# The first batch of an attention in chunks of 512, 288 and 288 tokens, and what of it stands ahead of the expert work

## The chip, the cores and the metric

The kernel runs on one core of a Trainium2 chip. The metric is the device time of one execution in microseconds (us). The parts of the core that matter here are TensorE (PE in the profile, with its weight loads as PEld), VectorE (DVE), ScalarE (ACT), GpSimd (POOL) and the queue of SyncE (SP), from which the transfers are issued. All data are float32.

## The reference

A polynomial-sketch attention feeds a mixture of eight experts whose weights come from eight rounds of Sinkhorn normalisation. Cut to what matters:

```python
def phi(x):                       # x: 4 batches, 4 heads, 1088 tokens, 32
    a = einsum('rd,bhsd->bhsr', S1, x)         # r = 8
    b = einsum('rd,bhsd->bhsr', S2, x)
    return einsum('bhsi,bhsj->bhsij', a, b)    # 64 features
q_p, k_p = phi(q), phi(k)
kv  = einsum('bhsf,bhsd->bhfd', k_p, v)        # over all keys of a batch
z   = sum(k_p, axis=2)
num = einsum('bhsf,bhfd->bhsd', q_p, kv)
den = einsum('bhsf,bhf->bhs', q_p, z)[..., None] + 1e-6
x   = num / den                                # 4352 tokens x 128
P   = exp(x @ w_gate - max), then 8 times: rows and columns normalised
out = sum over e of P[:, e] * (relu(x @ w1[e]) @ w2[e])   # 8 experts, 128 -> 1024 -> 128
```

The queries of a batch can be worked through in chunks of tokens, once the sums `kv` and `z` over all its keys are there. The experts' first products on a token need only that token's `x`; the router's weights `P` need all tokens.

## The kernel before

**The attention.** For each batch b, `transpose_k` and `transpose_q` (L276, L272) turn keys and queries with DVE transposes; `keys_ab` (L285), `keys_products` (three DVE products, L301) and `keys_sums` (72 small matmuls, L314) make the key sums, and `keys_kept` (L331) copies these from PSUM to the tile kvz in four small copies, by ACT and DVE in turn. The queries go in three chunks of 384, 352 and 352 tokens (`chunks`, L344). A chunk passes four functions: `query_products` (PE: eight matmuls on half the rows of the array each; ACT: two copies to qa), `multiply` (DVE: two products, L367), `fractions` (PE: eight matmuls into two banks, pd first and then pn, L377), and `divide` (DVE, in a row: a transpose of pd, an addition, a reciprocal, a transpose back, and the product with pn that writes the chunk's part of xT; L389 to L396).

**The expert work.** `steps()` (L979) is a generator. One of its steps is a first product (L800: four matmuls, of up to 480 tokens) with its relu on ACT (L804). Four steps are a block of two slices of the hidden layer by two tiles of tokens. Strassen's scheme with seven products replaces eight second products: in the first step of the next block DVE makes a double subtraction, in the step after that two single ones (`two`, L817), and from eight steps on (`LAG`, L767) the second products follow (L967: four matmuls a step). Steps 0 to 15 work on the first group of tokens, 0 to 511 of batch 0, in two tiles of 256 that take turns (`groups`, L531): even steps use tokens 0 to 255, odd ones 256 to 511. Step 16 starts the next group, of two tiles of 480 tokens: 512 to 991, and 992 to 1471, which reaches into batch 1.

**What sets the order.** The attention is written out by hand among the expert work. `fill(n)` (L1037) adds n to a debt and takes steps while it is over 0.25; a step of 256 tokens pays 256/480, one of 480 tokens pays 1:

```python
def fill(n):
    owed[0] += n
    while owed[0] > 0.25:
        owed[0] -= next(work)
```

In the first hand-written part (L1042 to L1061) DVE, PE and ACT take their work in the order of the code. From L1064 on this holds for DVE and PE alone; ACT, POOL and the queue of SP are put in order by the planner of the framework, as are the buffers. The four PSUM buffers of `bank()` (L94) serve the key sums, the fractions and the first products in turn; the query products of batch 0 use the four banks of the second products instead (L270). The weights of the first expert, w1 and w2, are loaded early (`first_w`, L262) on the queue of SP, behind keys, queries and values of batch 0 and the keys and queries of batch 1; the values of batch 1 come behind them.

Before the change, L1042 to L1091 take, per fill, these steps: 0 and 1; 2 and 3; 4 and 5; 6 and 7; 8; 9 and 10; 11 and 12; 13 and 14; then in `attention(1)` (L413) 15 and 16; and from 17 on one step per fill.

Of the kernel before, what the change touches and what calls it, by code (L numbers as in the profile page):

```python
# [10 lines left out]
F32 = mybir.dt.float32  # L11
# [39 lines left out]
def kernel(  # L51
# [13 lines left out]
    P = nc.NUM_PARTITIONS  # L65
    B, H, S, D = q.shape
# [25 lines left out]
    wk = early.enter_context(tc.tile_pool(name="wk", bufs=2))  # L92

    def bank():  # L94
        return aps.tile([P, 512], F32, tag="a", name="a")
# [141 lines left out]
    def projections():  # L237
        flat = raw.rearrange("p n d -> p (n d)")
        s12 = f64_to_f32(nc, consts, flat, (P, 2 * D)) if words == 2 else flat.bitcast(F32)
        st = consts.tile([P, 2, 32], F32, name="st")  # L240
        nc.vector.transpose(out=st.rearrange("p n r -> p (n r)"), in_=s12)
        nc.vector.tensor_tensor(wd, st[:, :, 0:R].unsqueeze(2).to_broadcast([P, 2, H, R]),
                                own.unsqueeze(1).unsqueeze(3).to_broadcast([P, 2, H, R]), op=Alu.mult)
        return st

    def repeated(st):
        for s in range(2):
            one = half[:, s:s + 1].unsqueeze(2).to_broadcast([P, R, R])
            nc.vector.tensor_tensor(wq[:, 0, s], st[:, 0, 0:R].unsqueeze(2).to_broadcast([P, R, R]), one, op=Alu.mult)
            nc.vector.tensor_tensor(wq[:, 1, s], st[:, 1, 0:R].unsqueeze(1).to_broadcast([P, R, R]), one,  # L250
                                    op=Alu.mult)
# [16 lines left out]
    def products_bank(b, i):  # L268

        return bank() if b else mps.tile([P, 512], F32, tag=f"s{i}", name="s")  # L270

    def transpose_q(b, lo=0, hi=S):  # L272
        if not lo:
            queries[b] = wk.tile([P, S], F32, tag="qT", name="qT")
        nc.vector.transpose(out=queries[b][:, lo:hi], in_=loaded[b][1].rearrange("p a d -> p (a d)")[:, lo:hi])  # L275

    def transpose_k(b):
        kx = loaded[b][0]
        kT = wk.tile([P, S], F32, tag="kT", name="kT")
        nc.vector.transpose(out=kT[:, 0:NT * P].rearrange("p (t c s) -> p c t s", c=4, s=32),  # L280
                            in_=kx[:, 0:4 * NT, :].rearrange("p (c t) d -> p c t d", c=4))
        nc.vector.transpose(out=kT[:, NT * P:S], in_=kx[:, 4 * NT:SA, :].rearrange("p a d -> p (a d)"))
        keys[b] = kT

    def keys_ab(b):  # L285

        kT = keys[b]
        ab = wk.tile([P, 2, NT + 1, H * R], F32, tag="ab", name="ab")
        pk = bank().rearrange("p (t n f) -> p t n f", t=NT, n=2)
        for t in range(NT):  # L290
            for s in range(2):
                sl = slice(64 * s, 64 * (s + 1))
                nc.tensor.matmul(pk[sl, t].rearrange("p n f -> p (n f)"), kT[:, P * t + 64 * s:P * t + 64 * (s + 1)],  # L293
                                 wdf, start=True, stop=True, tile_position=(0, 64 * s))
        nc.scalar.copy(ab[:, :, 0:NT, :], pk.rearrange("p t n f -> p n t f"))
        pr = bank()[0:64, 0:2 * H * R]
        nc.tensor.matmul(pr, kT[:, NT * P:S], wdf, start=True, stop=True, tile_position=(0, 0))
        nc.scalar.copy(ab[0:64, :, NT, :], pr.rearrange("p (n f) -> p n f", n=2))
        keys[b] = ab
# [31 lines left out]
    def keys_kept(b):  # L331
        pv = sums_of.pop(b)

        kvz = summed[b % 2]
        for i in range(2):
            for s in range(2):
                sl = slice(64 * s, 64 * (s + 1))
                if s:
                    nc.vector.tensor_copy(kvz[sl, :, i, s, :], pv[sl, i])
                else:  # L340
                    nc.scalar.copy(kvz[sl, :, i, s, :], pv[sl, i])
        keys[b] = kvz

    chunks = ((0, 384), (384, 736), (736, S))  # L344

    def query_products(b, c):

        lo, hi = chunks[c]
        n = hi - lo
        qT = queries[b]  # L350
        banks = [[products_bank(b, 2 * i + m) for m in range(2)] for i in range(2)]
        for m in range(2):
            for i in range(2):
                sl = slice(64 * i, 64 * (i + 1))
                nc.tensor.matmul(banks[i][m][:, 0:n], wqf[sl, m, :], qT[sl, lo:hi], start=True, stop=True,  # L355
                                 tile_position=(64 * i, 0))
        ph = []
        for i in range(2):
            qa = wk.tile([P, 384], F32, tag=f"qa{i}", name="qa")
            nc.scalar.copy(qa[:, 0:n], banks[i][0][:, 0:n])  # L360
            ph.append((qa, banks[i][1]))
        queries[b, c] = ph

    def multiply(b, c):
        n = chunks[c][1] - chunks[c][0]
        for qa, pb in queries[b, c]:
            nc.vector.tensor_tensor(qa[:, 0:n], qa[:, 0:n], pb[:, 0:n], op=Alu.mult)  # L367

    def fractions(b, c):

        n = chunks[c][1] - chunks[c][0]
        kvz = keys[b]
        ph = queries[b, c]
        pn, pd = bank(), bank()
        for t, m in ((pd, 1), (pn, 0)):
            for i in range(2):
                nc.tensor.matmul(t[64 * i:64 * (i + 1), 0:n], kvz[:, (i + m) % 2, i].rearrange("p h d -> p (h d)"),  # L377
                                 ph[i][0][:, 0:n], start=True, stop=True, tile_position=(0, 64 * i))
        queries[b, c] = pn, pd

    def divide(b, c):


        lo, hi = chunks[c]
        n = hi - lo
        nb = n // 32
        pn, pd = queries.pop((b, c))
        rd = wk.tile([P, 384], F32, tag="rd", name="rd")
        nc.vector.transpose(out=rd[:, 0:n], in_=pd[:, 0:n])  # L389
        rc = wk.tile([P, 12], F32, tag="rc", name="rc")[:, 0:nb]  # L390
        nc.vector.tensor_scalar_add(rc, rd[:, 0:n].rearrange("p (b r) -> p b r", r=32)[:, :, 0], 1e-6)
        nc.vector.reciprocal(rc, rc)
        rd = wk.tile([P, 384], F32, tag="rd", name="rd")
        nc.vector.transpose(out=rd[:, 0:n].rearrange("p (b r) -> p b r", r=32),
                            in_=rc.unsqueeze(2).to_broadcast([P, nb, 32]))
        nc.vector.tensor_tensor(xT[:, b * S + lo:b * S + hi], pn[:, 0:n], rd[:, 0:n], op=Alu.mult)  # L396
# [640 lines left out]
# [5 lines that stand above are left out]
    with tc.manual_schedule(engines={engines.DVE, engines.PE, engines.Activation}):  # L1042
        st = projections()
        transpose_k(0)
        keys_ab(0)
        repeated(st)
        transpose_q(0, 0, chunks[0][1])
        query_products(0, 0)
        for part_ in range(3):
            keys_products(0, part_)  # L1050
        keys_sums(0)
        multiply(0, 0)
        transpose_q(0, chunks[0][1])
        keys_kept(0)
        query_products(0, 1)
        fractions(0, 0)
        multiply(0, 1)
        divide(0, 0)
        fractions(0, 1)
        query_products(0, 2)  # L1060
        divide(0, 1)  # L1061
    counts = {1: (1, 1, 1, 1, 1, 1, 1, 1, 1), 2: (1, 1, 1, 1, 1, 1, 1, 1, 1, 1, 1, 2),
              3: (1, 1, 1, 1, 1, 1, 1, 1, 1, 1, 1, 1.25)}
    with tc.manual_schedule(engines={engines.DVE, engines.PE}):  # L1064
        fill(1)
        multiply(0, 2)
        fractions(0, 2)
        fill(1)
        transpose_k(1)
        divide(0, 2)  # L1070
        keys_ab(1)
        fill(1)
        transpose_q(1)
        load_kq(2)
        load_v(2)
        fill(1)
        keys_products(1, 0)
        query_products(1, 0)
        fill(1)
        keys_products(1, 1)  # L1080
        multiply(1, 0)
        fill(1)
        keys_products(1, 2)
        keys_sums(1)
        transpose_k(2)
        fill(1)
        keys_kept(1)
        fractions(1, 0)
        fill(1)
        for b in range(1, B):  # L1090
            for n, _ in zip(counts[b], attention(b), strict=True):  # L1091
                fill(n)
        for n in routing():
            fill(n)
        early.close()
        pools.append(ctx.enter_context(tc.tile_pool(name="late", bufs=2)))
        prepare_x(PLAIN)
        fill(8)
# [32 lines left out]
```

## Time and profile before

| | |
|---|---|
| median of four runs | 944.72 us (944.17 to 945.11) |
| the profiled execution | 944.47 us, of which the profile's span is 942.7 us |
| PE busy | 928.8 us (99%) |
| DVE busy | 702.8 us (75%) |
| ACT busy | 419.1 us (44%) |
| POOL busy | 192.5 us (20%) |
| TensorE clock granted, mean | 0.999 |

Times in the profile count from the span's start. In a line of the timeline the first number is the start, the second the duration (of a merged group, what it kept its engine busy), then engine, line, operation, tiles and shape; in brackets stands the engine's idle time before it and what ended that. A matmul's end is modelled and includes its way through the array, so two matmuls in a row overlap in the record, and the pace is read from starts. In a view by windows each entry is an engine's busy time in that stretch with its instructions in brackets, then the granted clock, the share of the DMA engines and their rate.

### The profile page before, as it was taken

What the parts mean: (1) busy time and instruction counts of PE and PEld (TensorE: products, weight loads), DVE (VectorE), ACT (ScalarE), POOL (GpSimd) and SP (SyncE); (2) the same over time, 40 slices, a digit from 0 to 9 for tenths busy, and PEclk for the clock granted to TensorE, in tenths of its full rate; (3) what the DMA queues carried; (4) which work ended last, traced back from release to release, by engine and by line L of the source; (5) the groups of instructions that cost most, each with busy time, mean ns of one, the idle gap of its engine ahead of it and who ended that gap; (6) DMA issues with size and microseconds to landing.
All of it is one profiled execution on the core that took longest, in us unless ns stands there. A gap on an engine that the chain in (4) does not pass through costs nothing.

```text
span 942.7 us, 18269 instructions
## 1 busy us (share of the span) xinstructions
PE 928.8 (99%) x7170; PEld 591.2 (63%) x7170; DVE 702.8 (75%) x1214; ACT 419.1 (44%) x894; POOL 192.5 (20%) x176
## 2 busy tenths in 40 slices
PE   8999999999999999999999999999999999999996
PEld 6553535566666666666666666666666666667864
DVE  7787579987778778676885756975767976668664
ACT  2444445555444454444544444544445444445443
POOL 2000000072456511040011100200110333311210
PEclk9999999999999999999999999999999999999999
DMA  6600000212434474444353434354344455443640
GB/s 191 188 1 1 2 1 1 68 62 85 129 107 124 121 237 130 144 142 159 122 154 116 169 128 130 124 164 149 120 132 139 155 175 185 155 168 92 188 131 12
DMA packets 86342, 113.07 MB, mean 120 GB/s; under 512 B 23888, under 2 KB 67920, under 8 KB 81904
## 3 DMA queue, kind: packets, MB, share of 16 engines
q1 hardware_dynamic: 85024, 111.74, 37.8%
q8 instruction: 56, 0.92, 0.4%
q10 hardware_dynamic: 1232, 0.16, 0.1%
q14 instruction: 30, 0.25, 0.1%
HBM read 99.03 MB, written 12.85 MB: 119 GB/s over the span
## 4 chain that ended last, share of the span: by engine, by line
PE 93%; DVE 5%; issue 1%; ACT 0%; DMA 0%; DVEq 0%; ACTq 0%
PE a L800 48%; PE s L967 41%; PE a L355 1%; PE a L377 1%; DVE hb L817 1%; PE a L324 1%; DVE hx L817 0%; DVE hx L862 0%; PE a L293 0%; DVE kp L309 0%; DMA raw<-in_S_dram 0%; DVE qa L367 0%; DVE kT L280 0%; DVE qT L275 0%; PE a L402 0%
## 5 line engine op out<-in xcount | busy, mean ns | idle before, releaser
L800 PE MATMUL a<-xe,w 128*64 128x256 f32 (+1 forms) x2560 | 525.6, 470 | 0.0
L804 ACT ACTIVATE hb<-a 128x256 f32<-128x256 f32 (+3 forms) x392 | 192.1, 492 | 257.6 <-PE a L800 232.6
L800 PEld LDWEIGHTS a<-xe,w 128*64 128x64 f32 x2560 | 227.6, 137 | 57.8
L804 ACT ACTIVATE hx<-a 128x256 f32<-128x256 f32 (+1 forms) x360 | 167.1, 464 | 213.0 <-PE a L800 192.6
L967 PE MATMUL s<-hb,ws 128*64 128x256 f32 (+2 forms) x1312 | 239.8, 400 | 0.0
L967 PE MATMUL s<-hx,ws 128*64 128x256 f32 x1280 | 209.3, 379 | 1.6 <-ACT f L679 1.1
L862 DVE TENSOR_TENSOR hb<-hb 128x512 f32<-128x512 f32 (+1 forms) x204 | 134.0, 666 | 101.1 <-ACT hb L804 96.7
L569 POOL TENSOR_TENSOR xe<-xT,xe 128x768 f32<-128x768 f32 (+2 forms) x41 | 84.2, 2054 | 567.5 <-DMA xe<-pT 387.3
L862 DVE TENSOR_TENSOR hx<-hx 128x512 f32<-128x512 f32 (+1 forms) x204 | 152.5, 756 | 62.0 <-ACT hx L804 56.8
L967 PEld LDWEIGHTS s<-hb,ws 128*64 128x64 f32 x1312 | 119.3, 137 | 101.7 <-issue 79.8
L967 PEld LDWEIGHTS s<-hx,ws 128*64 128x64 f32 x1280 | 116.1, 137 | 90.4 <-issue 67.4
L800 PE MATMUL a<-xT,w 128*64 128x480 f32 (+2 forms) x448 | 121.7, 506 | 1.1 <-DVE xT L396 0.9
L967 PE MATMUL s<-hb,w 128*64 128x256 f32 (+2 forms) x472 | 101.8, 423 | 1.0 <-DVE kept L627 1.0
L817 DVE TENSOR_TENSOR hb<-hb 128x480 f32<-128x480 f32 (+5 forms) x84 | 66.5, 795 | 13.8 <-PE s L967 7.2
L967 PE MATMUL s<-hx,w 128*64 128x256 f32 x384 | 69.6, 379 | 0.1
L800 PEld LDWEIGHTS a<-xT,w 128*64 128x64 f32 x448 | 44.2, 137 | 33.1 <-issue 18.1
L225 POOL TENSOR_TENSOR ws<-w 128x256 f32<-128x256 f32 (+1 forms) x70 | 60.4, 897 | 13.9 <-PE a L800 9.5
L967 PEld LDWEIGHTS s<-hb,w 128*64 128x64 f32 x472 | 44.9, 137 | 26.0 <-issue 11.6
L817 DVE TENSOR_TENSOR hx<-hx 128x256 f32<-128x256 f32 (+1 forms) x65 | 39.6, 614 | 24.3 <-ACT hx L804 17.9
L862 DVE TENSOR_TENSOR pqg<-hb 128x512 f32<-128x512 f32 x68 | 49.6, 770 | 0.0
L967 PEld LDWEIGHTS s<-hx,w 128*64 128x64 f32 x384 | 36.8, 137 | 8.0 <-DVE hx L817 0.5
L862 DVE TENSOR_TENSOR pqg<-hx 128x512 f32<-128x512 f32 x68 | 34.9, 553 | 0.0
(150 smaller groups left out, 484.4 us busy)
## 6 DMA issues: line engine op xcount, KB each, us to landing
w<-in_moe_w_dram SPq DMA_DIRECT2D x82, 512.0 KB, 5.4
ws<-ws SPq DMA_DIRECT2D x34, 1024.0 KB, 5.1
xe<-pT SPq DMA_DIRECT2D x34, 384.0 KB, 3.9
ws<-ws SPq DMA_DIRECT2D x12, 512.0 KB, 4.4
pb<-pT SPq DMA_DIRECT2D x6, 384.0 KB, 6.5
kx<-in_k_dram SPq DMA_DIRECT2D x4, 544.0 KB, 4.0
qx<-in_q_dram SPq DMA_DIRECT2D x4, 544.0 KB, 5.8
v<-in_v_dram SPq DMA_DIRECT2D x32, 64.0 KB, 4.5
```

The lines of the kernel that those rows point to most:

```text
L225: tc.keep_in_program_order(nc.gpsimd.tensor_tensor(ws[:, c:c + len(ns)], blocks(x), blocks(y), op=Alu.subtract if off else Alu.add))
L324: nc.tensor.matmul(pv[64 * s:64 * (s + 1), i], kp[0:n, H * t + h].rearrange("p i j -> p (i j)"), vx[0:n, slots[h], t, :], start=(t == 0 an ...
L355: nc.tensor.matmul(banks[i][m][:, 0:n], wqf[sl, m, :], qT[sl, lo:hi], start=True, stop=True, tile_position=(64 * i, 0))
L377: nc.tensor.matmul(t[64 * i:64 * (i + 1), 0:n], kvz[:, (i + m) % 2, i].rearrange("p h d -> p (h d)"), ph[i][0][:, 0:n], start=True, stop=T ...
L569: tc.keep_in_program_order(nc.gpsimd.tensor_tensor(out, x, pb, op=Alu.mult))
L800: nc.tensor.matmul(ph[sl], loaded_w[j][0][:, P * f + H2 * s:P * f + H2 * (s + 1)], sources[j][:, lo:hi], start=True, stop=True, tile_posit ...
L804: nc.scalar.activation(out=out, in_=ph, func=Act.Relu)
L817: nc.vector.tensor_tensor(out, a, b, op=Alu.subtract)
L862: nc.vector.tensor_tensor(out if not isinstance(out, tuple) else places(*out), places(*a), places(*b) if isinstance(b, tuple) else b, op=A ...
L967: nc.tensor.matmul(sums[g][i][H2 * s:H2 * (s + 1), n * place:n * (place + 1)], w, x, start=c == 1, stop=c == per, tile_position=(0, H2 * s))
```

## The change

Batch 0 gets chunks of its own: 512, 288 and 288 tokens instead of 384, 352 and 352. The other batches keep theirs. So `divide(0, 0)` now gives all of tokens 0 to 511, on which the first sixteen steps work.

In the first hand-written part, chunk 0 goes through to its `divide` with nothing of the other chunks between but the transpose of their queries and the query products of chunk 1; `fractions(0, 0)` now stands ahead of these query products on PE. The multiplication of chunk 1, its fractions and division, the query products of chunk 2 and the rest move into the second part, with fills between them. The fills ahead of `keys_ab(1)` are 0.5, 1, 0.5 and 0.5 instead of 1 and 1. Where the first query products and the division use tiles of 384 columns, these become 512 wide.

```diff
     chunks = ((0, 384), (384, 736), (736, S))
+    first_chunks = ((0, 512), (512, 800), (800, S))
+
+    def chunk(b, c):
+        lo, hi = (chunks if b else first_chunks)[c]
+        return lo, hi, hi - lo
...
-            qa = wk.tile([P, 384], F32, tag=f"qa{i}", name="qa")
+            qa = wk.tile([P, 512], F32, tag=f"qa{i}", name="qa")
...
-        rd = wk.tile([P, 384], F32, tag="rd", name="rd")
+        rd = wk.tile([P, 512], F32, tag="rd", name="rd")
...
-        transpose_q(0, 0, chunks[0][1])
+        transpose_q(0, 0, 512)
         query_products(0, 0)
         for part_ in range(3):
             keys_products(0, part_)
         keys_sums(0)
         multiply(0, 0)
-        transpose_q(0, chunks[0][1])
         keys_kept(0)
+        fractions(0, 0)
+        transpose_q(0, 512)
         query_products(0, 1)
-        fractions(0, 0)
-        multiply(0, 1)
         divide(0, 0)
-        fractions(0, 1)
-        query_products(0, 2)
-        divide(0, 1)
...
     with tc.manual_schedule(engines={engines.DVE, engines.PE}):
+        multiply(0, 1)
+        fill(0.5)
+        fractions(0, 1)
+        query_products(0, 2)
         fill(1)
+        divide(0, 1)
         multiply(0, 2)
+        fill(0.5)
         fractions(0, 2)
-        fill(1)
+        fill(0.5)
         transpose_k(1)
         divide(0, 2)
         keys_ab(1)
```

What follows `keys_ab(1)` is unchanged: six fills of 1 up to `attention(1)`.

More of the change, by code (lines that the diff above doesn't have):

```diff
@@ L344 @@
     chunks = ((0, 384), (384, 736), (736, S))
+    first_chunks = ((0, 512), (512, 800), (800, S))
+    def chunk(b, c):
+        lo, hi = (chunks if b else first_chunks)[c]
+        return lo, hi, hi - lo
     def query_products(b, c):
-        lo, hi = chunks[c]
-        n = hi - lo
+        lo, hi, n = chunk(b, c)
         qT = queries[b]
@@ L364, in multiply @@
     def multiply(b, c):
-        n = chunks[c][1] - chunks[c][0]
+        lo, hi, n = chunk(b, c)
         for qa, pb in queries[b, c]:
@@ L369, in fractions @@
     def fractions(b, c):
-        n = chunks[c][1] - chunks[c][0]
+        lo, hi, n = chunk(b, c)
         kvz = keys[b]
@@ L381, in divide @@
     def divide(b, c):
-        lo, hi = chunks[c]
-        n = hi - lo
+        lo, hi, n = chunk(b, c)
         nb = n // 32
         pn, pd = queries.pop((b, c))
-        rd = wk.tile([P, 384], F32, tag="rd", name="rd")
+        rd = wk.tile([P, 512], F32, tag="rd", name="rd")
         nc.vector.transpose(out=rd[:, 0:n], in_=pd[:, 0:n])
-        rc = wk.tile([P, 12], F32, tag="rc", name="rc")[:, 0:nb]
+        rc = wk.tile([P, 16], F32, tag="rc", name="rc")[:, 0:nb]
         nc.vector.tensor_scalar_add(rc, rd[:, 0:n].rearrange("p (b r) -> p b r", r=32)[:, :, 0], 1e-6)
         nc.vector.reciprocal(rc, rc)
-        rd = wk.tile([P, 384], F32, tag="rd", name="rd")
+        rd = wk.tile([P, 512], F32, tag="rd", name="rd")
         nc.vector.transpose(out=rd[:, 0:n].rearrange("p (b r) -> p b r", r=32),
```

## The prediction

> **What bounds the kernel now.** I read the page first, by slices and by the chain that ended last.
>
> ```profile
> PE   8999999999999999999999999999999999999996
> ...
> PEclk9999999999999999999999999999999999999999
> ...
> PE 93%; DVE 5%; issue 1%; ACT 0%; DMA 0%; DVEq 0%; ACTq 0%
> ```
>
> PE sets the time, at a full clock; its work is the same after the change (the same matmuls over the same columns). So the change can move the time only by PE's breaks, and nearly all breaks but the tail's are in the first slices. There I took the windows and PE's waits from 6 to 45 us:
>
> ```profile
> 18.00:20.00 2.00, 1.32 (x10) 0.38 (x6) 1.79 (x5) 1.19 (x3) 0.00 (x0) 1.00 0.54 119
> 26.00:28.00 2.00, 0.68 (x8) 0.38 (x6) 2.00 (x3) 0.62 (x2) 0.00 (x0) 1.00 0.86 268
> 36.00:38.00 2.00, 1.69 (x10) 1.02 (x11) 1.62 (x5) 0.20 (x1) 0.00 (x0) 1.00 0.92 275
> 80.00:100.00 20.00, 20.00 (x162) 9.54 (x161) 13.32 (x23) 10.41 (x21) 0.00 (x0) 1.00 0.01 1
> ...
> PE a L355 <- DVE qT L275: 1.3, 1, 1.3
> PE a L800 <- DVE xT L396: 0.9, 1, 0.9
> PE s L355 <- DVE qT L275: 0.5, 1, 0.5
> ```
>
> PE idles in the first three windows, while DVE is full (2.00 of 2.00 at 26 to 28); from 40 us on PE is full. So up to about 28 us DVE carries the chain, and PE waits for it. The timeline of DVE:
>
> ```profile
> 11.31 1.00 DVE L367 TENSOR_TENSOR qa<-qa,s 128x384 f32<-128x384 f32 x2
> 12.24 0.90 DVE L275 STREAM_TRANSPOSE qT<-qx 128x704 f32<-128x704 f32 x1
> 14.80 0.95 DVE L367 TENSOR_TENSOR qa<-qa,s 128x352 f32<-128x352 f32 x2 [0.92 <-PE s L355]
> 15.67 0.58 DVE L389 STREAM_TRANSPOSE rd<-a 128x384 f32<-128x384 f32 x1
> 17.91 0.54 DVE L389 STREAM_TRANSPOSE rd<-a 128x352 f32<-128x352 f32 x1
> 20.04 0.94 DVE L367 TENSOR_TENSOR qa<-qa,s 128x352 f32<-128x352 f32 x2
> 20.90 1.24 DVE L280 STREAM_TRANSPOSE kT<-kx 128x1024 f32<-128x1024 f32 x1
> 26.10 1.30 DVE L275 STREAM_TRANSPOSE qT<-qx 128x1088 f32<-128x1088 f32 x1
> ...
> 35.21 0.69 DVE L817 TENSOR_TENSOR hb<-hb 128x512 f32<-128x512 f32 x1 [1.64 <-PE s L967]
> 35.94 0.23 DVE L339 COPY kvz<-a 64x64 f32<-64x64 f32 x1
> ```
>
> From 11.31 to 26.10 DVE rests only 1.2 us: 0.92 ahead of 14.80 and 0.27 between two kvz copies. Two places on PE count:
>
> ```profile
> 18.67 0.65 PE L800 MATMUL a<-xT,w 128*64 128x256 f32 x4
> ...
> 27.55 1.56 PE L355 MATMUL a<-qT,wq 64*128 64x384 f32 x8 [1.32 <-DVE qT L275]
> ...
> 36.31 1.59 PE L377 MATMUL a<-qa,kvz 128*64 128x384 f32 x7 [0.34 <-DVE kvz L339]
> ```
>
> 27.55 is the first query product of batch 1. Both orders have done steps 0 to 7 there, so its new start is the measure of the first part.
>
> **Prices.** On DVE, from start to next start: a multiply is 0.46 at 384 (11.31, two in 0.93) and 0.435 at 352 (14.80 to 15.67), so by 0.0009 a column 0.58 at 512 and 0.375 at 288. A divide is 2.24 at 384 (15.67 to 17.91) and 2.13 at 352 (17.91 to 20.04): 2.68 at 512, 1.91 at 288. The query transposes of 384 and 704 columns took 0.58 and 0.90: 0.71 at 512, 0.77 at 576. The three chunks cost DVE the same together (divides 6.50 and 6.50). On PE a pair of query or fraction matmuls starts every 0.32 at 384 and 0.295 at 352: 0.43 at 512, 0.24 at 288, four pairs a call. A step is 0.43 without second products, 0.86 with them; its relu starts 0.70 after it and takes 0.38. Behind the half-row query products PE resumes 0.1 late; both orders change over equally often.
>
> **Wider first chunk.** The 512 transpose ends 0.13 later, at 8.1, where DVE then waits for ab until 8.70: free, and 0.13 less is left to do later. The four pairs end near 9.9, just ahead of the key sums, which waited for kp until 9.97: free; without that cover 0.4.
>
> **Chunk 0 alone.** DVE multiplies 11.31 to 12.47, but the key sums are ready at 12.78 as before, so with the transpose gone from here DVE rests 0.55, then 0.27 between kvz copies, which end at 13.75. Then the 576 transpose, to 14.52. `fractions(0, 0)` starts its second half at 13.79 on PE and its pd is there at 14.82: DVE rests 0.30. PE ends it at 15.51; query products of chunk 1: 15.61 to 16.58. Divide: 14.82 to 17.50; xT is seen at 17.64. Multiply of chunk 1: to 18.25.
>
> **Step 0 moves ahead.** It stood behind two fractions and chunk 2's query products; now it needs only xT (17.64) and w1. In the trace's record of semaphore updates the last of w1's sixteen landing counts comes at 17.88, and PE's wait for it (an EVENT_SEMAPHORE of L800) stands at 17.9. So step 0 runs 17.97 to 18.40 instead of at 18.67: a wait for w1 that cost nothing costs 0.3. Behind it in PE's queue stand `fractions(0, 1)` (18.41 to 19.38) and the query products of chunk 2 (19.48 to 20.45), then steps 1 to 3, to 21.84. Behind `fractions(0, 1)` waits DVE with `divide(0, 1)`: pd at 19.07, so DVE rests 0.82. Divide to 20.98, multiply of chunk 2 to 21.73.
>
> **A new wait.** The fill of 0.5 ahead of `transpose_k(1)` takes step 4, whose subtractions DVE has in order before the transpose. They need the relu of step 3, which starts at 21.41 + 0.70 and ends at 22.49: DVE rests 0.80. Behind it: subtraction 0.60, `transpose_k(1)` 1.29 (24.42), divide 1.91 (26.33), two subtractions 0.80, then the query transpose of batch 1 at 27.13 instead of 26.10. PE, out of work from 23.3, waits for kT until 24.4 and for qT until 28.58: **+1.03** at this place. DVE's rests are 0.55 + 0.27 + 0.30 + 0.82 + 0.80 = 2.74 against 1.2; the rest is the 0.13, and pauses inside the divide near 22.7 that I do not carry over. Bounds: if both of the larger rests vanish, -0.6; if each doubles, +2.6. I keep +1.03, since each is worked out between neighbouring rows.
>
> **What comes back.** The debt of fill gives after the change steps 0; 1, 2; 3; 4; 5, 6; 7; 8, 9; 10, 11; 12, 13; 14, 15; then 16, 17, 18 singly, the same as before from 17 on. So steps 11 and 12 no longer straddle the key sums of batch 1. Before, the subtraction of step 12 waited for step 11's second product (1.64), and held the kvz copies at 35.94 and PE's fractions at 36.31: PE lost 0.55, and 0.1 between their halves. Now step 11 is ahead of the key sums (33.57 to 35.92), DVE has subtracted and copied by 37.0, and PE comes to the fractions at 37.64: no break, **-0.65**. Bounds: 0 if the wait only changes place, -0.65. I take all, as 0.6 of slack is left.
>
> **Later.** In the routing one step of a fill changes side in six of the eight rounds (four instead of three, or the reverse). PE waits there once in the trace, 0.98 us at 134.9, for a DVE addition ahead of step 56's second products; that step stands behind the same round's DVE work in both orders. Bounds -1.0 and +1.0; I take 0, as rounds of three and of four steps both run without a break elsewhere. SP's transfers keep their code order; values and keys of batches 1 and 2 landed over a microsecond ahead of use. POOL's sums for step 8 ended at 23; needed at 30. The tail is untouched.
>
> **Sum.** +1.03 - 0.65 = +0.38 on the profiled execution: 944.47 (span 942.7 and 1.77 around it) becomes 944.85. That execution lies 0.25 under the median, so against it 944.72 + 0.38 = 945.1.
>
> **A rule against it.** The granted clock is 1.00 in the windows with PE's longest break (1.32 idle), and the new breaks, 1.4 ahead of step 0, 1.1 and 1.3, are hardly longer: nothing for the clock in the sum. The Trainium skill, "TensorE: Matmul & The Clock Gate", section "HAM oscillation — how this bites in real kernels", warns of bursts with waits between: an idle stretch of about 3.4 us halves the clock. No break here comes near that; by the page one such window would add about 1.7 us (an estimate from its figures).
>
> **Rivals.** A difference under 0.2% (1.9 us) is about what cannot be told from no change.
>
> *The lag stays* (+1.0, 945.8). DVE remains the bound after 28.6, and PE loses elsewhere what it saved at 36.3. For it: DVE is busy 2.00 and 1.97 of 2.00 in the windows after 28. Against: the next product that PE needs from it has 0.6 to spare.
>
> *Faster* (942.6). The waits for PE and relu are shorter than worked out and the bigger breaks close: from 12.5 to 36.7 PE's breaks sum to some 4.4 us; half of it is -2.1. For it: PE gets step 0 0.7 earlier. Against: DVE's work, in order, is no less, and it is the bound.
>
> *Slower: w1 is late* (947.1). Place: step 0, now the head of PE's queue, with the next fractions and so DVE's divide behind it: one for one. w2, issued next on the same queue, landed at 19.98 (POOL's first sum starts at 20.05); were w1 as late, +2.0 more. Past 0.2% from a landing at about 19.4 on. Against: nothing moves the transfers ahead of it.
>
> **How the numbers follow.** Forecast 0.63 (its own range 944.2 to 946.1), lag stays 0.16, faster 0.08, w1 late 0.07, and 0.06 for an order of ACT, POOL or SP from the planner that costs more than I can see. Of the faster case 0.06 pass 0.2%; of the slower two 0.12. So faster 0.06, same 0.82, slower 0.12. The range of 8 in 10 goes from 943.4 (half of the faster case) to 947.0 (w1 nearly as late as w2).
>
> **What would show it.** Step 0 near 18.0, the first query product of batch 1 near 28.6, no DVE wait of 1.6 us near 35, the fractions of batch 1 unbroken near 37.6, and `query_products(1, 1)` near 43.3 instead of 42.91. Wrong if that first product is ahead of 27.5 or behind 30, or if breaks on PE appear after 45 us.

## The result, and the profile after

The changed kernel takes 946.54 us (median; 945.4 to 948.62) beside 944.94 us (943.82 to 946.36) of the kernel before on the same chips: a ratio of 1.0017 [1.0013, 1.0022], so 1.6 us slower. That is inside the forecast range (943.4 to 947.0) and under the 0.2% that the forecast called "the same", but the forecast's own sum was +0.38. The profiled execution took 946.35 us, with a span of 944.6 us, 1.9 us more than that of before.

The page of the changed kernel, its rows of PE and of the granted clock in 40 slices, and its chain by engine:

```profile
PE   8899999999999999999999999999999999999996
...
PEclk9999999999999999999999999999999999999999
...
PE 95%; DVE 3%; ACT 1%; DMA 0%; issue 0%; SPq 0%; DVEq 0%; ACTq 0%
```

PE is still the bound at a full clock. The second slice (23.6 to 47.2 us) has gone from 9 to 8: the loss that a slice can show lies there. Windows of the changed kernel in that part (first PE's busy time, then PEld, DVE, ACT, POOL, the clock, the DMA share, GB/s):

```profile
18.00:20.00 2.00, 1.78 (x14) 1.19 (x16) 1.05 (x4) 0.38 (x1) 0.00 (x0) 1.00 0.61 120
24.00:26.00 2.00, 0.81 (x27) 0.84 (x29) 1.92 (x5) 0.29 (x1) 0.00 (x0) 1.00 0.92 346
36.00:38.00 2.00, 2.00 (x33) 1.43 (x29) 1.25 (x4) 0.68 (x3) 0.00 (x0) 1.00 0.15 41
```

At 18 us PE has gained (1.78 busy against 1.32), at 36 us too (2.00 against 1.69); at 24 us it stands idle for 1.19, with DVE nearly full (1.92 of 2.00). PE's waits from 6 to 45 us name what it stands for (us in total, times, longest):

```profile
PE a L293 <- DVE kT L282: 1.3, 1, 1.3
PE a L804 <- DVE qa L372: 1.2, 1, 1.2
PE a L360 <- DVE qT L275: 1.0, 1, 1.0
```

And the instructions behind it, of DVE and of PE, in the timeline of the changed kernel (in the changed code L804 is a first product, L821 a subtraction, L360 the query products, L382 the fractions, L393 to L400 a divide):

```profile
18.22 0.65 PE L804 MATMUL a<-xT,w 128*64 128x256 f32 x4 [1.22 <-DVE qa L372]
...
19.40 0.48 DVE L393 STREAM_TRANSPOSE rd<-a 128x288 f32<-128x288 f32 x1 [0.91 <-PE a L382]
...
22.92 0.97 DVE L821 TENSOR_TENSOR hb<-hb 128x512 f32<-128x512 f32 x1 [0.78 <-ACT hb L808]
23.81 1.23 DVE L280 STREAM_TRANSPOSE kT<-kx 128x1024 f32<-128x1024 f32 x1
...
29.14 1.56 PE L360 MATMUL a<-qT,wq 64*128 64x384 f32 x8 [1.03 <-DVE qT L275]
...
35.31 1.56 DVE L821 TENSOR_TENSOR hb<-hb 128x512 f32<-128x512 f32 x3
...
38.39 1.46 PE L382 MATMUL a<-qa,kvz 128*64 128x384 f32 x8
```

The view puts step 0's wait down to a multiplication, whose output step 0 does not read. In the trace's record of semaphore updates w1's last landing count came at 18.08, and step 0 starts 0.14 later; in the run with both repairs (below), where the view names w's transfer, the two are 17.93 and 18.07, also 0.14 apart.

Step 0 starts at 18.22 (worked out: 17.97); DVE waits 0.91 for pd of chunk 1 and 0.78 for the relu of step 3 (0.82 and 0.80); the wait of 1.64 us near 35 is gone, and the fractions of batch 1 run unbroken. All that is as forecast. But the first query product of batch 1 starts at 29.14 instead of 28.58.

To see where the rest arose, I take how late a step's first matmul starts against the same step in the trace of before (us):

| | 1st query product, batch 1 | step 17 | 24 | 26 | 60 | 68 | 73 | 77 | 80 | 120 | span's end |
|---|---|---|---|---|---|---|---|---|---|---|---|
| changed kernel | 1.59 | 0.75 | 0.78 | 1.12 | 1.11 | 1.05 | 1.29 | 1.79 | 1.99 | 1.72 | 1.90 |

Four movements: +1.6 in the head, -0.8 given back by step 17, +0.34 at step 25, and +0.9 between steps 68 and 80. Steps 68 to 80 run in the rounds of the routing: the part for which the prediction took 0. The 1.59 holds 0.19 that is no part of the change: DVE's first key transpose waits for the keys' transfer and starts at 5.77 instead of 5.58. From here on the head is measured from that transpose to the first query product of batch 1: 21.97 before, 23.37 after, **+1.40**.

### The profile page after: what moved, and what is told of

Same layout as the page of the kernel before. It is cut to its first block, busy times and chain, and to the rows that moved or that the text cites. A ratio compares the mean times of both kernels' runs of the same rounds, so it can differ in the third digit from the quotient of the medians.

```text
span 944.6 us, 18270 instructions
## 1 busy us (share of the span) xinstructions
PE 928.6 (98%) x7170; PEld 586.2 (62%) x7170; DVE 702.2 (74%) x1214; ACT 419.1 (44%) x894; POOL 192.8 (20%) x176
## 4 chain that ended last, share of the span: by engine, by line
PE 95%; DVE 3%; ACT 1%; DMA 0%; issue 0%; SPq 0%; DVEq 0%; ACTq 0%
PE a L804 49%; PE s L971 42%; PE a L382 1%; PE a L360 1%; PE a L324 1%; DVE hx L821 0%; PE s L360 0%; DMA kx<-in_k_dram 0%; PE a L293 0%; DVE hb L821 0%; DVE kT L280 0%; PE a L406 0%; DVE kept L631 0%; DVE hx L866 0%; DVE z L672 0%
## 5 line engine op out<-in xcount | busy, mean ns | idle before, releaser
L804 PE MATMUL a<-xe,w 128*64 128x256 f32 (+1 forms) x2560 | 525.5, 470 | 0.0
L804 PEld LDWEIGHTS a<-xe,w 128*64 128x64 f32 x2560 | 227.5, 137 | 57.4
L866 DVE TENSOR_TENSOR hb<-hb 128x512 f32<-128x512 f32 (+1 forms) x204 | 135.9, 676 | 96.1 <-ACT hb L808 91.6
L866 DVE TENSOR_TENSOR hx<-hx 128x512 f32<-128x512 f32 (+1 forms) x204 | 150.6, 748 | 67.4 <-ACT hx L808 62.6
L804 PE MATMUL a<-xT,w 128*64 128x480 f32 (+2 forms) x448 | 118.9, 506 | 1.5 <-DVE qa L372 1.2
L821 DVE TENSOR_TENSOR hb<-hb 128x480 f32<-128x480 f32 (+5 forms) x84 | 65.7, 783 | 12.1 <-PE s L971 5.8
L804 PEld LDWEIGHTS a<-xT,w 128*64 128x64 f32 x448 | 42.0, 137 | 35.2 <-issue 22.0
L821 DVE TENSOR_TENSOR hx<-hx 128x256 f32<-128x256 f32 (+1 forms) x65 | 39.4, 610 | 24.5 <-ACT hx L808 17.6
```

The source lines that it names most:

```text
L804: nc.tensor.matmul(ph[sl], loaded_w[j][0][:, P * f + H2 * s:P * f + H2 * (s + 1)], sources[j][:, lo:hi], start=True, stop=True, tile_posit ...
L821: nc.vector.tensor_tensor(out, a, b, op=Alu.subtract)
L866: nc.vector.tensor_tensor(out if not isinstance(out, tuple) else places(*out), places(*a), places(*b) if isinstance(b, tuple) else b, op=A ...
```

## The experiments

The theory after the result: (a) DVE's wait for the relu of step 3 is what the head costs; (b) what comes back stems from step 11 ahead of the key sums; (c) the 0.9 in the routing stems from the debt of `fill` alone: the fills ahead of `keys_ab(1)` sum to 2.5 instead of 2, and so one step changes side in the rounds. The rivals: the wider first chunk itself costs; w1 is late for step 0; the order of step 0 ahead of the fractions costs; the difference in the routing is only how late the head comes in. Each time below is a median against the kernel before run alongside.

### The sizes alone

The kernel before, in its own order, with the new chunks:

```diff
+    first_chunks = ((0, 512), (512, 800), (800, S))
...
-        transpose_q(0, 0, chunks[0][1])
+        transpose_q(0, 0, 512)
...
-        transpose_q(0, chunks[0][1])
+        transpose_q(0, 512)
```

> The order of before, with the chunks of 512, 288 and 288 tokens for batch 0. If the change's loss lies in its order (theory): DVE's work and rests stay, the first query product of batch 1 comes within 0.3 us of 27.55, and the time is that of before, -0.3 to +0.3 us. If it lies in the sizes (rival: the large first chunk holds up the key sums or PSUM): that product at 28.5 or later and +1 us or more.

Measured: 944.64 against 945.38 us, ratio 0.9995 [0.9986, 1.0004]. The interval leaves room for a cost of 0.4 us at most, so the sizes don't carry the loss; what the change costs is its order. The head is 22.32, 0.35 over before and so a little past the 0.3 expected; one stretched instruction holds 0.75 of it (below).

### The debt put back

The changed kernel with its debt back at that of before from batch 1 on:

```diff
-    counts = {1: (1, 1, 1, 1, 1, 1, 1, 1, 1), ...
+    counts = {1: (0.5, 1, 1, 1, 1, 1, 1, 1, 1), ...
```

> The changed kernel, with 0.5 instead of 1 for the first fill in attention(1): the same steps up to step 53, but the debt of before from there, so that the routing takes its steps in the rounds of before. If the 0.9 us that the changed kernel loses between step 64 and step 80 come from the steps that changed their round (theory): that loss is gone, step 80 lags before by 1.1 us as step 60 did, and the time is 0.6 to 0.9 us below the changed kernel's, about +0.8 over before. If they come from the lag itself, which meets the transfers or ACT at another time (rival): step 80 lags by 2.0 us and the time stays at +1.6.

Measured: 945.61 against 945.38 us, ratio 1.0002 [0.9993, 1.0010], against 1.0017 of the changed kernel. The lag stays at 0.96 from step 24 to step 80: the 0.9 is gone, and so is the 0.34 at step 25, which (c) doesn't account for ("The rest", below); some +0.8 over before was expected, and +0.2 was measured. Of the 1.4 us between the two ratios 0.9 is the routing, so about half of the loss in the profiled execution (0.9 of 1.9) was in the term that I had set to 0.

### Step 4 behind the key transpose

```diff
-        fill(0.5)
         transpose_k(1)
+        fill(0.5)
         divide(0, 2)
```

> The changed kernel with the second fill of 0.5 (step 4 and its subtraction) behind transpose_k(1) instead of ahead of it. If DVE's wait of 0.78 us for a relu carries the chain (theory): transpose_k(1) starts at about 22.2 instead of 23.8, the first query product of batch 1 at 28.3 instead of 29.14, and the time falls by 0.7 to 0.9 us. If PE loses it again elsewhere (rival): that product moves, but the time stays within 0.3 us of the changed kernel's.

Measured: 945.95 against 945.38 us, ratio 1.0010 [1.0001, 1.0019]; the head is 22.72 instead of 23.37. DVE in the timeline of this run:

```profile
22.33 1.24 DVE L280 STREAM_TRANSPOSE kT<-kx 128x1024 f32<-128x1024 f32 x1
...
23.61 0.65 DVE L821 TENSOR_TENSOR hb<-hb 128x512 f32<-128x512 f32 x1
```

The transpose that PE needs starts at 22.33 instead of 23.81, the subtraction follows without a wait, and PE gets its work earlier. So (a) holds for 0.65 of the head's 1.40, or 0.84 once the stretches listed in the last section are taken off; the rest of the head's cost is not the relu's. The times, 1.0010 against 1.0017, point the same way, but their intervals overlap. The steps 68 to 80 still lose 0.9 (lag 0.41 at step 60, 1.31 at step 80), though the head comes in 0.7 earlier: how late the head is doesn't decide the routing.

### What comes back, alone

The kernel before, with half a unit of fill brought forward so that step 11 stands ahead of the key sums, and taken off later:

```diff
         query_products(1, 0)
-        fill(1)
+        fill(1.5)
         keys_products(1, 1)
...
-    counts = {1: (1, 1, ...
+    counts = {1: (0.5, 1, ...
```

> The kernel before with 1.5 instead of 1 for the fill behind the first query products of batch 1, and 0.5 instead of 1 for the first fill in attention(1): steps 8 to 15 are taken half a unit earlier, as in the changed kernel, and the debt is that of before from step 17 on. If the change's gain near 36 us is real (theory): no DVE wait of 1.64 us ahead of the key sums' copies, PE's fractions of batch 1 start without a break, and the time is 0.4 to 0.7 us below before. If the wait only changes place (rival): within 0.2 us of before.

Measured: 944.45 against 945.38 us, ratio 0.9990 [0.9982, 0.9999]. DVE in its timeline:

```profile
34.14 1.56 DVE L817 TENSOR_TENSOR hb<-hb 128x512 f32<-128x512 f32 x3
35.80 0.23 DVE L339 COPY kvz<-a 64x64 f32<-64x64 f32 x1
```

The wait of 1.64 us ahead of the subtraction is gone, with nothing else of the change in the kernel. `query_products(1, 1)` comes 36.61 after the first key transpose instead of 37.33: -0.72. The head of this run is 0.19 longer than before, so between the two places it gains 0.91; the prediction had -0.65. (b) stands, and it needs none of the rest of the change.

### Both repairs

The changed kernel with the debt put back and step 4 behind the transpose.

> The changed kernel with both of the last edits: step 4 behind transpose_k(1), and 0.5 for the first fill in attention(1). If the two losses are separate and add (theory): first query product of batch 1 at about 22.7 us after the first key transpose (23.4 changed, 22.0 before), no growth of the lag from step 56 to step 80, and the time 1.2 to 1.8 us below the changed kernel's, 0.5 us under to 0.3 us over before. If they overlap (rival): no better than either alone, +0.6 or more over before.

Measured: 944.72 against 945.11 us, ratio 0.9997 [0.9988, 1.0006]. Head 22.27, lag -0.09 at steps 26 to 80. Taken together the two edits undo the whole loss: the head still costs 0.30, and what comes back covers it.

### The fractions ahead of step 0

The kernel of the last run, and:

```diff
         multiply(0, 1)
-        fill(0.5)
         fractions(0, 1)
+        fill(0.5)
         query_products(0, 2)
```

> As the kernel with both edits, and fractions(0, 1) ahead of the first fill of 0.5, so that step 0 stands behind it on PE. If step 0 at the head of PE's queue is what makes DVE wait 0.9 us for the fractions (theory): that wait falls to 0.3 to 0.5, the first query product of batch 1 comes 0.4 to 0.6 us earlier than with both edits alone, and the time falls by 0.2 to 0.6 us. If PE, not DVE, decides by then (rival): the wait falls and the time stays within 0.2 us.

Measured: 945.08 against 945.11 us, ratio 1.0000 [0.9992, 1.0009]. DVE's wait at the divide of chunk 1:

```profile
19.54 0.48 DVE L393 STREAM_TRANSPOSE rd<-a 128x288 f32<-128x288 f32 x1 [0.79 <-PE a L382]
```

It is 0.79 with step 0 in front of the fractions (the run before) and 0.79 with step 0 behind them. So the prediction's 0.82 was right in size but wrong in cause: I had put it to step 0. It is the way from `multiply` through PE's fractions back to `divide`: 1.60 us from the multiply's start to the divide's in both, of which the multiply is 0.81. In the kernel before, DVE had other chunks' work for that time. The head is 22.65, 0.38 later than in the run before instead of 0.4 to 0.6 earlier: the query products of chunk 2, now behind both, start at 20.35 instead of 19.64, and DVE multiplies chunk 2 from 21.69 instead of 21.19.

### The debt alone, on the kernel before

```diff
-    counts = {1: (1, 1, 1, 1, 1, 1, 1, 1, 1), ...
+    counts = {1: (1.5, 1, 1, 1, 1, 1, 1, 1, 1), ...
```

> The kernel before with 1.5 instead of 1 for the first fill in attention(1): the same steps up to step 53, but the debt of the changed kernel, so its rounds of the routing. If the steps that change their round are the cost (theory): the lag is 0 up to step 60, grows by 0.6 to 0.9 us by step 80, and the time is 0.4 to 1.0 us above before. If the cost needs the changed kernel's lag too (rival): within 0.3 us of before.

Measured: 946.03 against 945.11 us, ratio 1.0008 [1.0000, 1.0017]. Head and batch 0 are as before, and the lag goes from -0.26 at step 68 to 0.71 at step 80. (c) is shown from the other side: half a unit of debt, more than 100 us earlier, costs 0.9 to 1.0 us in the routing, without the changed kernel's late head.

What happens there is read in one round. The changed kernel, DVE and PE:

```profile
166.30 0.66 DVE L505 TENSOR_REDUCE cs<-p 128x8 f32<-128x280 f32 x1
166.88 1.33 DVE L821 TENSOR_TENSOR hb<-hb 128x480 f32<-128x480 f32 x2
...
166.67 0.57 PE L971 MATMUL s<-hb,ws 128*64 128x480 f32 x1
...
167.58 0.62 PE L971 MATMUL s<-hb,ws 128*64 128x480 f32 x1
```

The same two subtractions in the kernel before, and the first instruction of the round:

```profile
165.04 1.34 DVE L817 TENSOR_TENSOR hb<-hb 128x480 f32<-128x480 f32 x2
...
167.65 0.21 DVE L508 RECIPROCAL cr<-a 128x8 f32<-128x8 f32 x1
```

And in the kernel before with the larger debt:

```profile
165.00 0.66 DVE L501 TENSOR_REDUCE cs<-p 128x8 f32<-128x280 f32 x1
165.58 1.34 DVE L817 TENSOR_TENSOR hb<-hb 128x480 f32<-128x480 f32 x2
```

Before, the subtractions stand ahead of a round's six small instructions; with more debt they stand behind them, and these hold DVE for 2.7 us (164.20 to 166.88). The second product that needs the first subtraction's output starts 0.91 after its neighbour, where the pace is 0.40. PE's waits don't list it, since the other half of the columns runs on and PE counts as busy (3.00 of 3.00 from 166 to 169 us); it stands among the waits of the weight loads of the changed kernel, from 165 to 169 us:

```profile
PEld s L971 <- DVE hb L821: 0.4, 1, 0.4
```

This place is 0.5 of the 0.9 (lag 1.29 at step 73, 1.79 at step 77). Most of the 0.24 ahead of it arises shortly before this round, where PE as a whole does stand idle, in the changed kernel at 161.27:

```profile
161.27 0.62 PE L971 MATMUL s<-hb,w 128*64 128x480 f32 x1 [0.32 <-DVE kept L631]
```

All five traces with the larger debt have this break of 0.32 (the changed kernel, the changed kernel again, step 4 behind the transpose, w1 earlier, and the kernel before with more debt), and none of the other eight has it. The 0.20 behind it wasn't followed to single instructions.

### w1 earlier

The changed kernel, with the transfers of keys and queries of batch 1 behind those of the first expert's weights:

```diff
     load_v(0)
-    load_kq(1)
...
     first_w = load_w(0)
+    load_kq(1)
     load_v(1)
```

> The changed kernel with the first expert's weights loaded ahead of the keys and queries of batch 1. If the landing of w1 holds step 0, and through it the chain (theory of the prediction): w1 lands by 15 us, step 0 starts 0.05 us after xT, 0.2 to 0.4 us earlier than in the changed kernel, and the time falls by 0.2 to 0.4 us. If DVE is held by its own chain from multiply over fractions to divide (theory since step 0 was put behind the fractions without gain): step 0 starts earlier, but the first query product of batch 1 stays within 0.2 us and the time within 0.3 us of the changed kernel's.

The weights do land earlier: POOL's first sum of w2 starts at 17.91 instead of 20.43, and step 0 is released by xT. Measured: 945.99 against 944.73 us, ratio 1.0013 [1.0004, 1.0022]; the head is 23.31. And the changed kernel again, beside it:

> The changed kernel once more, beside the others on one chip: +1.2 to +2.0 us over before; the growth of the lag between steps 72 and 80 (0.9 us) comes again, since it is in the order; the 0.3 us at step 25 may not, if it depends on when DVE's additions fall between the two halves of the array.

Measured: 946.60 against 944.73 us, ratio 1.0016 [1.0007, 1.0025]; head 23.44. Step 0 is released by w1 in some executions and by xT in others: in the first trace of the changed kernel w1's last landing count came at 18.08, and the divide of chunk 1 started 1.72 after the multiply; in the second it came at 17.51, and the divide started after 1.60, as in both runs with the repairs. So w1 cost 0.12 in the first execution and nothing in the second. The earlier w1 gains no more than that, and its run has other shifts that cancel: the queries of batch 0 land later (+0.27 by the key products), and the subtraction of step 4 is shorter (0.69 instead of 0.97). It doesn't carry the loss.

### The sizes with what comes back

The new chunks in the order of before, with the two edits of fill of "What comes back, alone".

> The order of before with the chunks of 512, 288 and 288 tokens, 1.5 for the fill behind the first query products of batch 1 and 0.5 for the first in attention(1). If the sizes cost nothing and the fill gains (theory): 0.4 to 1.0 us below before, as with the fill alone. If the two want the same rest of PE (rival): no better than the sizes alone, within 0.3 us of before.

Measured: 943.96 against 945.11 us, ratio 0.9990 [0.9982, 0.9999].

> The order of before with the chunks of 512, 288 and 288 tokens, 1.5 for the fill behind the first query products of batch 1 and 0.5 for the first in attention(1), once more: 0.6 to 1.4 us below before and 2.2 to 3.2 us below the changed kernel if its lead was no accident; within 0.4 us of before if it was.

The same once more, beside another set of runs: 943.89 against 944.73, ratio 0.9989 [0.9980, 0.9998]. So this version is some 1.0 us faster than the kernel before and some 2.6 faster than the changed one. Nearly all of its gain is that of the two fills (0.9990 with the old chunks); that the new chunks add to it is not shown.

## Why the prediction was right or wrong

**The verdict and the range** held: +1.6 us is under the 1.9 us of "the same" (the interval reaches past it, to 1.0022), and 946.54 is inside. The size didn't hold: +0.38 against +1.6, and 946.54 lies outside the forecast's own range of 944.2 to 946.1. The upper end of 947.0 had been set for a late w1, which did not happen, so that the time lies inside is partly luck.

**Wider first chunk: free.** Right, by the run with the sizes alone.

**Chunk 0 alone, step 0, the new wait.** The waits were placed rightly and their sum was nearly right: 0.35 + 0.27 + 0.36 + 0.91 + 0.78 = 2.67 on DVE, against 2.74. The wait "behind step 0" has another cause (the fractions run). w1 costs 0.12 or nothing instead of 0.3, since the fractions behind step 0 wait for the multiply's end anyway, which came at 18.49 instead of 18.25 (0.19 of it the later start). The sum of +1.03 missed +0.37 all the same. Of this 0.3 is one phrase: "pauses inside the divide near 22.7 that I do not carry over". A pause of 0.30 was in the trace of before (an addition of 0.47 instead of 0.17). It doesn't go: it falls on whatever DVE does beside POOL's sums, which is now the subtraction of step 4: 0.97, where the row of before had 0.69. With the 0.3 added back the step would have read 1.33, against 1.40.

**What comes back.** Right in its mechanism, and larger than forecast: -0.65 forecast, -0.83 measured between the two places (1.40 to 0.57), -0.91 alone. The rival "the lag stays" is out.

**Later: "I take 0, as rounds of three and of four steps both run without a break elsewhere".** This is the step that failed: +0.9. I looked for breaks in which PE as a whole stands idle. Of what is lost there 0.5 is one column half waiting while the other runs, which PE's busy time doesn't show; shortly before, the whole PE does stand idle, for 0.32. That is a new break after 45 us, which the prediction had named as a sign of being wrong. I had the bound (+1.0) and chose the middle of it without looking at where DVE's subtractions stand in the order of a round. The -0.25 between steps 80 and 120 isn't tied to the debt: two traces with the debt of before fall by 0.26 and 0.27 there, and the second trace of the changed kernel by 0.13.

**The rest**: +0.34 at step 25. It came in the changed kernel and in several others (0.33 with the sizes alone), and not in some others of the same order at that place (0.08 in the second trace of the changed kernel, 0.01 with the debt put back). The traces show where it comes from: near 48 to 52 us a DVE instruction falls beside POOL's sums and takes longer (the last section has more on this), and DVE, which PE waits for at step 25, carries the delay there. The changed kernel's POOL and the addition of a divide, which takes 0.17 alone:

```profile
48.80 0.73 POOL L188 TENSOR_TENSOR ws<-w 128x256 f32<-128x256 f32 x1
...
49.01 0.55 DVE L395 TENSOR_SCALAR rc<-rd 128x11 f32<-128x11 f32 x1
```

And the same addition in the second trace of the changed kernel:

```profile
48.88 0.26 DVE L395 TENSOR_SCALAR rc<-rd 128x11 f32<-128x11 f32 x1
```

So DVE loses 0.38 and 0.09 there, and from step 17 to step 26 the lag grows by 0.37 and 0.08. With the sizes alone the addition takes 0.28 and a subtraction behind it 1.69 instead of 1.14, 0.66 in all, and the lag grows by 0.64. In all twelve traces the two agree to 0.03. One kernel shows 0.38 in one execution and 0.09 in another, so the order alone doesn't fix it. This is a reading of traces; no run took POOL's sums away from this place.

**The rivals.** The slower one, w1 late, did not happen (last count at 18.08 and 17.51, far from 19.4). None of my rivals was the order inside the routing, though the change's debt reaches there; it should have been the slower rival.

So the +1.9 of the profiled execution is made of +0.19 (later start, no part of the change), +1.40, -0.83, +0.34, +0.9, -0.25 by step 120, and +0.2 after it, which wasn't followed (sum 1.95).

## What to carry to other kernels

When fills of work are moved among hand-ordered stages, follow the debt to the end: half a unit more near 20 us set the order of two subtractions and six small instructions at 165 us. Where a matmul engine runs two halves side by side, as here, its busy share and its list of waits don't show a half that waits; compare the start of each step with the same step of the other trace. And a chain that goes from one engine to the other and back (multiply, fractions, divide) needs other work of the first engine beside it: chunks that go through alone have none.

## What was not expected of the hardware

Some DVE instructions with inputs in SBUF, here a subtraction of two tiles and the small addition of a divide, are stretched, without any idle time ahead of them, when they start beside a running sum of POOL. Timelines of the changed kernel's two executions and of the one with w1 earlier; first the changed kernel's POOL, beside its subtraction shown above (22.92, 0.97):

```profile
22.61 0.73 POOL L189 TENSOR_TENSOR ws<-w,ws 128x256 f32<-128x256 f32 x1
```

The changed kernel again:

```profile
22.49 0.73 POOL L189 TENSOR_TENSOR ws<-w,ws 128x256 f32<-128x256 f32 x1
...
22.64 1.12 DVE L821 TENSOR_TENSOR hb<-hb 128x512 f32<-128x512 f32 x1 [0.79 <-ACT hb L808]
```

With w1 and w2 earlier, POOL has done its sums by 20.8:

```profile
20.09 0.72 POOL L188 TENSOR_TENSOR ws<-w,ws 128x256 f32<-128x256 f32 x1
...
22.99 0.69 DVE L821 TENSOR_TENSOR hb<-hb 128x512 f32<-128x512 f32 x1 [0.78 <-ACT hb L808]
```

The same subtraction takes 0.69 alone, 0.97 when it starts 0.42 before POOL's sum ends, and 1.12 when it starts 0.58 before. The transposes (0.48) and the products with an input from PSUM (0.45 and 0.46) kept their times beside the same sums. The divide's addition went from 0.17 to 0.47 (before), 0.66 (step 4 behind the transpose) and 0.92 (the sizes alone) in this way. The Trainium skill, "SBUF — State Buffer", section "SBUF: two separate sides", has a rule for it: VectorE and GpSimd share one pair of SBUF ports, held by one instruction until its end, and a VectorE instruction with two SBUF inputs or in a two-port mode must wait for it. The traces agree with it to about 0.1: by the page the two subtractions would have ended at 24.01 and 23.89, an estimate (POOL's end and 0.67, the middle of the 0.65 to 0.69 that the subtraction takes without POOL), and they ended at 23.89 and 23.76. The addition has one input in SBUF; no run shows whether it runs in a two-port mode.

Taken off (the subtraction counted over 0.67, the addition over 0.17), the stretch also clears up the scatter of the heads (us):

| | head | stretch | head without it |
|---|---|---|---|
| before | 21.97 | 0.30 | 21.67 |
| before, fills moved | 22.16 | 0.48 | 21.68 |
| before, more debt | 21.69 | 0 | 21.69 |
| sizes alone | 22.32 | 0.75 | 21.57 |
| sizes and fills, both runs | 21.73, 22.36 | 0, 0.61 | 21.73, 21.75 |
| changed, both runs | 23.37, 23.44 | 0.30, 0.45 | 23.07, 22.99 |
| changed, debt put back | 23.40 | 0.19 | 23.21 |
| changed, w1 earlier | 23.31 | 0 | 23.31 |
| step 4 behind the transpose | 22.72 | 0.49 | 22.23 |
| both repairs | 22.27 | 0 | 22.27 |
| and the fractions ahead of step 0 | 22.65 | 0 | 22.65 |

So the order of the change costs the head 1.3 to 1.5 (the run with w1 earlier holds its 0.27 of later queries besides), and 0.6 of that remains with step 4 behind the transpose. Some 0.45 of this 0.6 is, as an estimate, DVE's rests that stay there (0.35 + 0.27 + 0.35 + 0.79 = 1.76 against 1.2 before, less the 0.13 that the wider first transpose saves later); no run took these rests away. The same stretch shows once more near 416 to 424 us, where subtractions of 0.69 take 2.0 to 2.3 beside POOL's sums of about 2 us: in three executions with four of these (the changed kernel again, step 4 behind the transpose, before with the fills moved) PE waits 0.3 to 0.6 for them, and the lag grows by 0.81, 0.76 and 0.57 there; with three it grew by 0.02 in the first trace of the changed kernel and by 0.37 in the run with the fractions ahead. No run took POOL's sums away, so this last part is a reading of traces and not an experiment.
